# 24 of 1164 feed-forward chunks by way of ScalarE and GpSimd, and steps that run across block ends

## The chip, the core and the metric

The kernel runs on one core of a Trainium2 chip. A core has five engines with a queue each, and each works its queue in order: TensorE (PE, with its weight loads shown apart as PEld), VectorE (DVE), ScalarE (ACT), GpSimd (POOL) and SyncE (SP, which here only starts transfers). Work passes between them by semaphores. Matmul results land in PSUM, which has 8 banks of 512 float32 values per partition; GpSimd works on SBUF alone here. The metric is the time of one execution in device microseconds; "the time before" is the median of several executions.

## What is computed

`x` has 4 batches of 12416 rows of 128 values. The first half is attention by way of 32 inducing rows, the second a gated feed-forward layer with 1536 hidden units on all 49664 rows:

```
h   = softmax(scale * I @ x^T) @ x          # per batch: 32 rows, from all rows of x
y   = softmax(scale * x @ h^T) @ h          # per row of x: 32 weights
out = (sigmoid(y @ w_gate) * (y @ w_val)) @ w_out
```

The sigmoid is taken as `0.5 * (tanh(z / 2) + 1)`; the 0.5 is multiplied in at the output.

## The kernel before

**Stages.** A batch has 97 chunks of 128 rows, in 6 groups of 16 and one chunk left over. Stage 1 (`plan_stage1`) makes `h` of a batch: scores on PE, maximum on VectorE, exp on ScalarE, a transpose by DMA, a sum on PE; `plan_combine` joins the groups on GpSimd. Since `y` is only 32 weights per row times `h`, the kernel multiplies `h` into the two feed-forward weights once per batch (`hw`, 32 rows instead of 128, four copies on the four groups of 32 rows of the array). Stage 2 (`plan_stage2`) makes the 32 weights of each row of a group: scores on PE into the side bank, a copy out by ScalarE (`s2_take`, L455), the row maximum and the subtraction on GpSimd (`s2_lower_pool`, L457 to L475), exp on ScalarE (L479), and on GpSimd the sum (`s2_sum_pool`), the reciprocal (`s2_inverse_pool`) and the product `a2n` (`s2_spread`, L533); a DMA turns it (`a2r`).

**Feed-forward.** Four chunks of rows (512 columns) are a *block*: 96 blocks and one of the four left-over chunks. For each block the 1536 hidden units are taken in 12 chunks of 128 (97 x 12 = 1164 feed-forward chunks, numbered `j` in a block). A *step* has 2 or 1 of them, in turn, so a block is 8 steps; two steps, three chunks, are a *slot* here. For step `t`: `gate_fill` multiplies on PE into the gate banks, `gate` is the tanh on ScalarE from PSUM to SBUF (L809), `hidden_mm(st, "v")` fills the value banks, and the *product* on VectorE (L818) makes `u = (tanh + 1) * value` from SBUF and PSUM. `product(t)` emits the value fill of `t`, then the gate fill of `t + 2`, then the product; the product of a 2-chunk step is made to wait for the gate fill of `t + 2` (L829). A fill of a chunk has K = 32, and lies on one of four row groups by `j % 2` and by gate or value.

**Banks.** The 2-chunk step has two banks for its gate and two for its value, the 1-chunk step one and one, the output accumulator `acc` one, and all the rest (stage 1, stage 2, combining) shares the eighth, tag `m`: the side bank.

**Order.** It is written out by hand. `at(slot, make, late)` puts the work of the stages into slots: early work goes behind the first step of the slot, late work behind the second, ahead of `project`. `project` (L837) emits the output matmuls of finished products, four of 128 columns per chunk, 3 chunks in a slot, or 4 where more than 3 wait; it stops at the end of a block, where ScalarE copies the accumulator out (L865) and SP writes it (L867). Slots are counted from `base[b]`, the first of batch `b`. Buffers come from rotating pools: a tile's first writer waits for the last reader of the tile that had its buffer.

Of the kernel before, what the change touches and what calls it, by code (L numbers as in the profile page):

```python
# [9 lines left out]
F32 = mybir.dt.float32  # L10
F16 = mybir.dt.float16
BF16 = mybir.dt.bfloat16
AF = mybir.ActivationFunctionType
ALU = mybir.AluOpType
# [3 lines left out]
P = 128  # L18
# [7 lines left out]
def kernel(  # L26
# [29 lines left out]
    s1p = ctx.enter_context(tc.tile_pool(name="s1p", bufs=4))  # L56
    s2p = ctx.enter_context(tc.tile_pool(name="s2p", bufs=2))
    up = ctx.enter_context(tc.tile_pool(name="up", bufs=6))
    tp = ctx.enter_context(tc.tile_pool(name="tp", bufs=4))
    op = ctx.enter_context(tc.tile_pool(name="op", bufs=4))  # L60

# [106 lines left out]
    def at(slot, make, late=False):  # L170
        plan.setdefault((slot, late), []).append(make)
# [39 lines left out]
    def s1_exp(b, s, s1):  # L211
        ng, w, R = s1_dims(s)
        nm, l1, col = s1_col(b, s)
        a1T = s1p.tile([P, 512], F16, tag="a1T")
        nc.scalar.activation(  # L215
            out=a1T[0:R, 0 : w * P],
            in_=s1[0:R, 0 : w * P],
            func=AF.Exp,
            bias=nm[0:R, col],
            **({} if b else dict(accum_out=l1[0:R, col])),  # L220
        )
        return a1T
# [329 lines left out]
    def plan_stage2(b, c, score, take, weigh, far=None, soon=False):  # L552
        st = {}
        n = GC + (NLO if far is not None else 0)

        def bank():
            st["s2"] = ps.tile([P, GC, m], F32, tag="m", name="s2_ps")

        def room():
            st["sc"] = s2p.tile([P, GC + NLO, m], F32, tag="sc", name="sc", bufs=1)  # L560

        def one():
            room()
            bank()
            s2_score(b, 0, 0, NLO, st["s2"], True)

        def half(j0, whole):
            if j0 == 0:
                bank()
            s2_score(b, c, j0, j0 + GC // 2, st["s2"], whole)  # L570
            if soon and j0:
                st["hl"] = s2_max(GC, st["s2"])

        def lower():
            if far is None:
                room()
            s2_take(st["sc"], 0, GC, st["s2"])
            s2_lower_pool(n, st["sc"])

        def exp():  # L580
            st["e"] = s2_exp(GC, st["s2"], *st["hl"]) if soon else s2_exp_low(n, st["sc"])

        def total():
            st["sme"] = s2_sum_pool(n, st["e"])

        def spread():
            rs = (s2_inverse if soon else s2_inverse_pool)(n, st["sme"])
            st["a2n"] = s2_spread(n, st["e"][:, 0:n, :], rs, nc.gpsimd)

        def turn():  # L590
            s2_turn_dma(b, c, GC, st["a2n"], "a2r")
            if far is not None:
                s2_turn_dma(b, 0, NLO, st["a2n"], "a2l", GC)

        if far is not None:
            at(far, one)
            at(far + 1, lambda: s2_take(st["sc"], GC, NLO, st["s2"]))
        at(score, lambda: half(0, False))
        at(score + 1, lambda: half(GC // 2, not soon))
        if not soon:  # L600
            at(take, lower, late=True)
        at(weigh, exp, late=True)
        at(weigh + 1, total)
        at(weigh + 3, spread)
        at(weigh + (5 if soon else 8 if far is None else 7), turn)
# [160 lines left out]
    s2_turn_dma(0, NLO + 2 * BC, GC - 2 * BC, a2n_c, "a2r")  # L766


    steps = []
    blocks = []  # L770
    first_step = {}
    for b in range(B):
        for s in range(NG):
            first_step[(b, s)] = len(blocks) * 2 * NJ // 3
            blocks += [[(b, groups[s][0] + k, BC)] for k in range(0, GC, BC)]
    blocks.append([(b, 0, NLO) for b in range(B)])
    for i in range(len(blocks)):
        for j in range(0, NJ, 3):
            steps.append(dict(block=i, j0=j, cnt=2))
            steps.append(dict(block=i, j0=j + 2, cnt=1))  # L780
    NST = len(steps)

    def hidden_mm(st, what):
        pt = ps.tile([P, st["cnt"], 512], F32, tag=f"{what}{st['cnt']}", name=f"{what}_ps")
        for k in range(st["cnt"]):
            j = st["j0"] + k
            r = 32 * (j % 2 + (2 if what == "v" else 0))
            col = 0
            for b, c, nb in blocks[st["block"]]:
                a2r, o = a2[(b, c)]  # L790
                st[what + "end"] = nc.tensor.matmul(  # L791
                    pt[:, k, col : col + nb * P],
                    hw[b][r : r + 32, j // 2, :],
                    a2r[r : r + 32, o : o + nb, :].rearrange("p j t -> p (j t)"),
                    start=True,
                    stop=True,
                )
                col += nb * P
        st[what] = pt

    def gate_fill(t):
# [9 lines left out]
    def product(t):  # L811
# [14 lines left out]
        if st["cnt"] == 2 and 4 <= t < NST - 2:  # L826
# [3 lines left out]
                u.ins, steps[t + 2]["gend"].ins.name, AFTER, reason="tanh, gate fill, product"  # L830
            )

    acc = [None]
    queue = [(t, k) for t in range(NST) for k in range(steps[t]["cnt"])]
    queue.reverse()

    def project(upto, now, room):  # L837
        while queue and queue[-1][0] < upto and room > 0:
            t, k = queue.pop()
            st = steps[t]  # L840
            j = st["j0"] + k
            if j == 0:
                acc[0] = [ps.tile([P, BC, C], F32, tag="acc", name="acc_ps")]
                if st["block"] == len(blocks) - 1:
                    acc[0].append(ps.tile([P, BC, C], F32, tag="m", name="acc_ps"))
            for i in range(BC):
                nc.tensor.matmul(  # L847
                    acc[0][(i // 2) % len(acc[0])][:, i, :],
                    st["u"][:, k, ts(i, P)],
                    wo16[:, j, :],  # L850
                    start=(j == 0 and i in ((0, 2) if len(acc[0]) > 1 else (0,))),
                    stop=(j == NJ - 1),
                    skip_group_check=True,
                )
            room -= 1
            if t == NST - 1:
                o32 = op.tile([P, BC, C], F32, tag="o32")
                nc.scalar.mul(out=o32[:, 0:2], in_=acc[0][0][:, 0:2], mul=0.5)
                nc.sync.dma_start(ov0[:, 0, 0:2, :], o32[:, 0:2])
                nc.vector.tensor_scalar_mul(out=o32[:, 2:4], in0=acc[0][1][:, 2:4], scalar1=0.5)  # L860
                nc.scalar.dma_start(ov0[:, 0, 2:4, :], o32[:, 2:4])
            elif j == NJ - 1:
                block = blocks[st["block"]]
                o32 = op.tile([P, BC, C], F32, tag="o32")
                nc.scalar.mul(out=o32[:], in_=acc[0][0][:], mul=0.5)  # L865
                b, c, nb = block[0]
                nc.sync.dma_start(ov[b, :, c : c + nb, :], o32[:])  # L867
                if now < NST:
                    return


    base = [first_step[(b, 0)] // 2 for b in range(B)]
    for b in range(B):
        o = base[b]
        more = b + 1 < B

        if b == 0:
            plan_stage2(0, groups[1][0], o, None, o + 3, soon=True)
            plan_stage2(0, groups[2][0], o + 5, o + 7, o + 18)
        for s in range(3 if b == 0 else 2, NG - 1):  # L880
            k = o + 16 * s - 28
            plan_stage2(b, groups[s][0], k, k + 2, k + (14 if more else 10))
        plan_stage2(b, groups[NG - 1][0], o + 56, o + 58, o + 66, far=o + 52)
        if not more:
            continue
        early = (
            [(9, (16, 17, 17)), (13, (18, 19, 19))]
            if b == 0
            else [(8, (15, 16, 17)), (12, (18, 19, 19))]
        )  # L890
        later = [(24, (31, 31, 31)), (28, (35, 35, 35)), (40, (47, 48, 49)), (44, (50, 51, 51))]
        for s, (score, total) in enumerate(early + later + [(32, (43, 43, 43))]):
            plan_stage1(b + 1, s, o + score, [o + e for e in total])
        plan_combine(b + 1, o + 52, o + 55, [(o + 72, o + 74), (o + 80, o + 82)])
        plan_stage2(b + 1, groups[0][0], o + 67, o + 70, o + 78)
        plan_stage2(b + 1, groups[1][0], o + 84, o + 86, o + 94)
        for g in range(NS):
            when = 3 * g if b else 5 * g if g < NG else 12
            at(o + when, lambda b=b, g=g: x_transpose_dma(b + 1, g))
            if b == 0 and 3 <= g < NG:  # L900
                at(o + (3, 14, 17)[g - 3], lambda g=g: x_load(1, g))
        if b + 2 < B:
            for g in range(NG):
                at(o + (24, 33, 42, 60, 60, 82)[g], lambda b=b, g=g: x_load(b + 2, g))
# [56 lines left out]
```

## Time and profile before

| | |
|---|---|
| median of 3 runs | 729.52 us (729.26 to 730.78) |
| profiled execution, span from first to last instruction | 728.4 us |
| product, 1024 columns | 388 instructions, 1208 ns mean |
| product, 512 columns | 387, 673 ns |
| tanh, 1024 and 512 columns | 388 of 1032 ns, 388 of 606 ns |
| output copy, 128x512 | 96, 607 ns |
| GpSimd a2n, 128x2048 | 19, 3610 ns |
| GpSimd reciprocal (pow), 128x16 | 18, 2935 ns |
| VectorE's idle time in front of its products | 5.1 us |
| ScalarE's idle time in front of its tanh | 33.3 us |

A row of the page's groups reads: line, engine, operation, output<-inputs, shapes, count, then busy time and mean of one, then the idle time of the engine just before them with what ended it. A row of the timeline reads: start, length, engine, line, operation, count, and in brackets the idle time before it with its releaser. A row of the stretches has the stretch, its length, the busy time (and count) of PE, PEld, DVE, ACT and POOL, then the granted clock of TensorE, the DMA share and the GB/s. Records of one engine overlap by some 0.1 us, since a record begins before the one ahead of it has drained: the distance between starts tells what an instruction costs, not the record's length.

### The profile page before, as it was taken

To read this page: it belongs to the slowest core of one execution; us is meant where nothing else is said; L and a number is where in the kernel's file an instruction comes from. 1 tells how busy PE (TensorE), PEld (TensorE's weight loads), DVE (VectorE), ACT (ScalarE), POOL (GpSimd) and SP (SyncE) were. 2 spreads that over 40 slices of the span, in tenths; PEclk is the share of its full clock that TensorE was granted. 3 is DMA by queue.
4 is the path that set the end of the run, shared out by engine and by line. 5 is a ranking of instruction groups with operands and counts; after the bars stand their busy time and mean duration, and the time that the engine had idled before them with its cause. 6 is when DMAs were issued, how large, how long until landed. Compare 5 with 4: busy or idle time off the path is not lost.

```text
span 728.4 us, 21430 instructions
## 1 busy us (share of the span) xinstructions
PE 645.6 (89%) x8406; PEld 392.7 (54%) x8406; DVE 706.0 (97%) x873; ACT 675.1 (93%) x1011; POOL 419.0 (58%) x702
## 2 busy tenths in 40 slices
PE   6798888999998989999988989999999899898887
PEld 4354555555555555555555555555555555555555
DVE  3898999999999999999999999999999999999998
ACT  4688999999999999999999999999999999999996
POOL 3553836688764548488757275387865665636200
PEclk9799999999999999999999999999999999999999
DMA  9899565143547372326169530320222122121211
GB/s 172 145 161 201 98 118 103 45 103 90 91 100 168 68 147 67 81 60 133 48 114 162 103 90 31 87 69 36 75 60 74 45 60 68 43 67 45 60 45 45
DMA packets 117749, 65.19 MB, mean 89 GB/s; under 512 B 101360, under 2 KB 102032, under 8 KB 117648
## 3 DMA queue, kind: packets, MB, share of 16 engines
q1 hardware_dynamic: 111936, 49.81, 30.4%
q0 software_dynamic: 5440, 13.90, 11.2%
q8 instruction: 65, 1.06, 0.6%
q14 instruction: 36, 0.29, 0.2%
q10 hardware_dynamic: 272, 0.13, 0.1%
HBM read 27.80 MB, written 25.43 MB: 73 GB/s over the span
## 4 chain that ended last, share of the span: by engine, by line
DVE 55%; issue 24%; PE 11%; ACT 5%; DMA 3%; DVEq 1%; POOL 0%; ACTq 0%; POOLq 0%
DVE u L818 53%; ACT t L809 5%; PE acc_ps L847 4%; PE v_ps L791 3%; DMA a<-a1T 2%; DVE nm L202 2%; PE xt_ps L612 1%; DVEq L818 1%; DMA xn<-in_x_dram 1%; PE hp_ps L250 1%; PE s_ps L190 0%; PE g_ps L791 0%; ACT a1T L215 0%; PE s_ps L418 0%; PE aT_ps L228 0%
## 5 line engine op out<-in xcount | busy, mean ns | idle before, releaser
L818 DVE SCALAR_TENSOR_TENSOR u<-t,v_ps 128x1024 f16<-128x1024 f16 (+1 forms) x777 | 675.5, 939 | 5.1 <-PE g_ps L791 4.7
L809 ACT ACTIVATE t<-g_ps 128x1024 f16<-128x1024 f32 (+1 forms) x776 | 593.7, 819 | 33.3 <-ACT t L809 17.5
L791 PE MATMUL v_ps<-a2r,hwt 32*128 32x512 f16 (+1 forms) x1188 | 294.4, 372 | 65.6 <-DVE u L818 64.6
L847 PE MATMUL acc_ps<-wo,u 128*128 128x128 f16 x4656 | 329.6, 221 | 0.0
L847 PEld LDWEIGHTS <-u 128*128 128x128 f16 x4656 | 262.8, 98 | 88.8 <-issue 87.8
L791 PE MATMUL g_ps<-a2r,hwt 32*128 32x512 f16 (+1 forms) x1188 | 297.5, 378 | 0.0
L791 PEld LDWEIGHTS <-hwt 32*128 32x128 f16 x2400 | 91.1, 91 | 197.7 <-issue 153.4
L487 POOL TENSOR_TENSOR sum<-e 128x256 f32<-128x256 f16 (+1 forms) x23 | 15.4, 671 | 148.2 <-ACT e L479 144.2
L533 POOL TENSOR_TENSOR a2n<-e,rs 128x2048 f16<-128x2048 f16 (+2 forms) x24 | 86.2, 3593 | 6.7 <-PE g_ps L791 2.8
L511 POOL TENSOR_TENSOR near<-sme,minus 128x16 f32<-128x16 f32 (+1 forms) x22 | 65.2, 2963 | 1.8
L865 ACT ACTIVATE o<-acc_ps 128x512 f32<-128x512 f32 x96 | 58.3, 607 | 0.0
L466 POOL TENSOR_SCALAR rise<-rise 128x256 f32<-128x256 f32 (+6 forms) x110 | 51.1, 464 | 9.7
L465 POOL TENSOR_TENSOR rise<-sc 128x256 f32<-128x256 f32 (+1 forms) x22 | 16.2, 738 | 38.9 <-ACT sc L455 38.7
L467 POOL TENSOR_TENSOR top<-top,rise 128x128 f32<-128x128 f32 (+3 forms) x88 | 28.3, 321 | 7.3
L487 POOL TENSOR_TENSOR sum<-sum 128x128 f32<-128x128 f32 (+3 forms) x92 | 28.3, 307 | 7.2
L465 POOL TENSOR_TENSOR rise<-top 128x128 f32<-128x128 f32 (+3 forms) x88 | 27.1, 308 | 6.9
L470 POOL TENSOR_TENSOR sc<-sc,top 128x512 f32<-128x512 f32 (+1 forms) x22 | 23.9, 1084 | 1.7
L418 PEld LDWEIGHTS <-xT 128*128 128x128 f16 x388 | 13.4, 97 | 12.2 <-issue 12.2
L418 PE MATMUL s_ps<-hT,xT 128*128 128x32 f16 x388 | 18.2, 179 | 0.3 <-DVE hT L315 0.3
L467 POOL TENSOR_TENSOR top<-sc,rise 128x256 f32<-128x256 f32 (+1 forms) x22 | 16.3, 740 | 1.8
L250 PE MATMUL hp_ps<-xn,a 128*32 128x128 f16 x388 | 14.2, 225 | 2.9 <-DMA a<-a1T 2.6
L215 ACT ACTIVATE a1T<-s_ps,nm 128x512 f16<-128x512 f32 (+1 forms) x24 | 15.1, 628 | 1.7 <-DVE nm L202 1.7
(118 smaller groups left out, 235.9 us busy)
## 6 DMA issues: line engine op xcount, KB each, us to landing
out_dram<-o SPq DMA_DIRECT2D x96, 256.0 KB, 2.3
xn<-in_x_dram POOLq DMA_DIRECT2D x19, 512.0 KB, 8.1
xn<-in_x_dram POOLq DMA_DIRECT2D x4, 544.0 KB, 6.3
a2r<-a2n SPq DMA_TRANSPOSE x29, 4.4
xn<-in_x_dram POOLq DMA_DIRECT2D x1, 384.0 KB, 14.6
wg<-in_moe_w_gate_dram POOLq DMA_DIRECT2D x1, 384.0 KB, 4.4
wv<-in_moe_w_val_dram POOLq DMA_DIRECT2D x1, 384.0 KB, 5.4
wo<-in_moe_w_out_dram POOLq DMA_DIRECT2D x1, 384.0 KB, 5.5
```

The costliest lines, as they stand in the source:

```text
L418: nc.tensor.matmul(s2[:, j, :], xT[b][:, c + j, :], hT16[b][:], start=(j == 0), stop=whole and j == j1 - 1, skip_group_check=True,)
L465: nc.gpsimd.tensor_tensor(out=r, in0=far, in1=near, op=ALU.subtract)
L466: nc.gpsimd.tensor_scalar_max(out=r, in0=r, scalar1=0.0)
L467: nc.gpsimd.tensor_tensor(out=top[:, 0:n, 0:w], in0=near, in1=r, op=ALU.add)
L487: nc.gpsimd.tensor_tensor(out=d[:, 0:n, :], in0=src[:, :, 0:w], in1=src[:, :, w : 2 * w], op=ALU.add)
L511: nc.gpsimd.tensor_tensor(out=near[:, 0:n], in0=sme[:, 0:n], in1=minus1[:, 0:n], op=ALU.pow)
L533: eng.tensor_tensor(out=a2n[:, 0:n, :, :], in0=e.unsqueeze(2).to_broadcast((P, n, 4, m)), in1=rs.unsqueeze(2).unsqueeze(3).to_broadcast((P ...
L791: st[what + "end"] = nc.tensor.matmul(pt[:, k, col : col + nb * P], hw[b][r : r + 32, j // 2, :], a2r[r : r + 32, o : o + nb, :].rearrange ...
L809: st["tanh"] = nc.scalar.activation(out=st["t"][:], in_=st["g"][:], func=AF.Tanh, scale=0.5)
L818: u = nc.vector.scalar_tensor_tensor(out=st["u"][:, :, c:e], in0=st["t"][:, :, c:e], scalar=1.0, in1=st["v"][:, :, c:e], op0=ALU.add, op1= ...
L847: nc.tensor.matmul(acc[0][(i // 2) % len(acc[0])][:, i, :], st["u"][:, k, ts(i, P)], wo16[:, j, :], start=(j == 0 and i in ((0, 2) if len( ...
L865: nc.scalar.mul(out=o32[:], in_=acc[0][0][:], mul=0.5)
```

## The change

24 chunks leave the steps. For each, `plan_aside` puts a gate fill into the side bank at one slot, a tanh to a float32 tile `tx` on ScalarE and an addition of 1 on GpSimd (late in that slot); at a second slot a value fill into the side bank, a copy to a float32 tile `vx` on ScalarE and a product on GpSimd to a tile `ux`. `tx` and `vx` have one buffer each, `ux` two. The projection of such a chunk comes at the end of its block. Of the 24, 3, 4, 4 and 13 are in the four batches; `aside` lists (gate slot, value slot, block from the batch's first). The steps then take the remaining 1140 chunks in order, three to a slot, whatever block they are in, and the slots of the stages are counted from the shifted starts of the batches (0, 95, 190, 284 in place of 0, 96, 192, 288). The pools of tanh tiles, output tiles and `a1T` go from 4 buffers to 3.

```diff
-    tp = ctx.enter_context(tc.tile_pool(name="tp", bufs=4))
-    op = ctx.enter_context(tc.tile_pool(name="op", bufs=4))
+    tp = ctx.enter_context(tc.tile_pool(name="tp", bufs=3))
+    op = ctx.enter_context(tc.tile_pool(name="op", bufs=3))
+    xp = ctx.enter_context(tc.tile_pool(name="xp", bufs=2))
...
-        a1T = s1p.tile([P, 512], F16, tag="a1T")
+        a1T = s1p.tile([P, 512], F16, tag="a1T", bufs=3)
...
+    usual = [(60, 65, 17), (76, 88, 23), (90, 92, 24)]
+    aside = [
+        list(usual),
+        [(0, 2, 2)] + usual,
+        [(0, 2, 2)] + usual,
+        [(0, 2, 2), (8, 10, 3), (16, 18, 6), (24, 26, 7), (32, 34, 10), (40, 42, 11)]
+        + [(48, 50, 14), (60, 62, 17), (68, 70, 19), (72, 74, 19), (77, 79, 21), (81, 83, 22)]
+        + [(85, 87, 23)],
+    ]
+    kept = [NJ] * len(blocks)
+    for b in range(B):
+        for k, (g, v, i) in enumerate(aside[b]):
+            kept[first_block[(b, 0)] + i] -= 1
...
-    for i in range(len(blocks)):
-        for j in range(0, NJ, 3):
-            steps.append(dict(block=i, j0=j, cnt=2))
-            steps.append(dict(block=i, j0=j + 2, cnt=1))
+    chunks = [(i, j) for i in range(len(blocks)) for j in range(kept[i])]
+    steps = []
+    for k in range(0, len(chunks), 3):
+        steps.append(dict(chunks=chunks[k : k + 2], cnt=2))
+        steps.append(dict(chunks=chunks[k + 2 : k + 3], cnt=1))
...
+    def plan_aside(gate_slot, value_slot, i, j):
+        st = {}
+
+        def fill(what):
+            st[what] = ps.tile([P, 512], F32, tag="m", name=f"side_{what}")
+            hidden_chunk(st[what][:], i, j, what)
+
+        def gate_take():
+            st["t"] = xp.tile([P, 512], F32, tag="tx", name="tx", bufs=1)
+            nc.scalar.activation(out=st["t"][:], in_=st["g"][:], func=AF.Tanh, scale=0.5)
+            nc.gpsimd.tensor_scalar_add(out=st["t"][:], in0=st["t"][:], scalar1=1.0)
+
+        def value_take():
+            v = xp.tile([P, 512], F32, tag="vx", name="vx", bufs=1)
+            nc.scalar.copy(out=v[:], in_=st["v"][:])
+            uside[(i, j)] = xp.tile([P, 512], F16, tag="ux", name="ux16")
+            nc.gpsimd.tensor_tensor(
+                out=uside[(i, j)][:], in0=st["t"][:], in1=v[:], op=ALU.mult
+            )
+
+        at(gate_slot, lambda: fill("g"))
+        at(gate_slot, gate_take, late=True)
+        at(value_slot, lambda: fill("v"))
+        at(value_slot, value_take, late=True)
...
-    queue = [(t, k) for t in range(NST) for k in range(steps[t]["cnt"])]
+    queue = []
+    for t in range(NST):
+        for k, (i, j) in enumerate(steps[t]["chunks"]):
+            queue.append((t, k, i, j))
+            if j == kept[i] - 1:
+                queue += [(t, None, i, e) for e in range(kept[i], NJ)]
...
+        for g, v, i, j in aside[b]:
+            plan_aside(o + g, o + v, i, j)
```

`hidden_chunk` is the inner loop of `hidden_mm`, taken out: one matmul for each part of the block, of one chunk `j`.

## The prediction

> **What bounds the kernel now.** I read the engine shares and the chain of waits of the page, then the groups by shape, then the timeline of single instructions around 409 us. A *slot* is two steps, three chunks: one product of 1024 columns and one of 512.
>
> ```profile
> PE 645.6 (89%) x8406; PEld 392.7 (54%) x8406; DVE 706.0 (97%) x873; ACT 675.1 (93%) x1011; POOL 419.0 (58%) x702
> ...
> DVE 55%; issue 24%; PE 11%; ACT 5%; DMA 3%; DVEq 1%; POOL 0%; ACTq 0%; POOLq 0%
> ...
> L818 DVE SCALAR_TENSOR_TENSOR u<-t,v_ps 128x1024 f16<-128x1024 f16 x388 | 468.5, 1208 | 3.4 <-PE g_ps L791 3.0
> L818 DVE SCALAR_TENSOR_TENSOR u<-t,v_ps 128x512 f16<-128x512 f16 x387 | 260.4, 673 | 1.7 <-PE g_ps L791 1.7
> ...
> 407.49 1.20 DVE L818 SCALAR_TENSOR_TENSOR u<-t,v_ps 128x1024 f16<-128x1024 f16 x1
> ...
> 409.22 1.20 DVE L818 SCALAR_TENSOR_TENSOR u<-t,v_ps 128x1024 f16<-128x1024 f16 x1
> ...
> 408.75 0.39 PE L791 MATMUL v_ps<-a2r,hwt 32*128 32x512 f16 x2
> 409.35 0.37 PE L791 MATMUL v_ps<-a2r,hwt 32*128 32x512 f16 x1
> 409.67 0.84 PE L847 MATMUL acc_ps<-wo,u 128*128 128x128 f16 x12
> 410.48 0.39 PE L791 MATMUL v_ps<-a2r,hwt 32*128 32x512 f16 x2
> ...
> 409.66 0.67 PEld L847 LDWEIGHTS <-u 128*128 128x128 f16 x12 [0.23 <-issue]
> 410.44 0.14 PEld L791 LDWEIGHTS <-hwt 32*128 32x128 f16 x5
> ...
> 409.24 1.51 ACT L809 ACTIVATE t<-g_ps 128x1024 f16<-128x1024 f32 x2 [0.21 <-ACT t L809]
> 410.64 0.60 ACT L865 ACTIVATE o<-acc_ps 128x512 f32<-128x512 f32 x1
> 411.12 1.04 ACT L809 ACTIVATE t<-g_ps 128x1024 f16<-128x1024 f32 x1
> ```
>
> VectorE looks like the bound at 97%. The single rows show that it is one member of a ring. The 1024-column product starts at 407.49 and ends at 408.69; only then can PE refill its bank pair (408.75, 0.39 us, with the gate fill of the next step beside it), and the next such product starts at 409.22. One turn is 409.22 - 407.49 = 1.73 us, and 388 turns are 671 us of the 728.4. Nothing in this ring runs ahead: a delay of PE or of ScalarE at the fill is added to the end and is not won back. How near the two are to delaying it: PE's last projection weights are in at 409.66 + 0.67 = 410.33 and the fill's weights load at 410.44, so PE has 0.11 us to spare in a slot. ScalarE ends its tanh at about 409.24 + 1.03 = 410.27 and the fill that waits for it starts at 410.48: 0.21 us. One output copy (410.64) pushes the next tanh from 409.24 + 1.73 = 410.97 to 411.12, which these 0.21 us still hide.
>
> **What is gained.** 24 chunks are 8 slots (the changed program has 380 of the 1024-column products, not 388): 8 x 1.73 = 13.8 us. No other term shortens the ring, so this is all there is to win.
>
> **GpSimd's queue, and one buffer.** The side chunk's tanh goes into tx, of which there is one; it is free when GpSimd has multiplied the chunk before. Counted in slots from a batch's base, every batch but the last has a side chunk with gate 76 and value 88, and the next gate at 90. In GpSimd's order that multiply stands behind the row maximum of the group whose scores ScalarE copies out in slot 86. In the second batch that stretch is:
>
> ```profile
> 365.17 0.72 POOL L465 TENSOR_TENSOR rise<-sc 128x256 f32<-128x256 f32 x1 [3.05 <-ACT sc L455]
> ...
> 372.68 1.07 POOL L470 TENSOR_TENSOR sc<-sc,top 128x512 f32<-128x512 f32 x1
> ...
> 371.73 1.51 ACT L809 ACTIVATE t<-g_ps 128x1024 f16<-128x1024 f32 x2 [0.21 <-ACT t L809]
> ```
>
> GpSimd is taken until 373.75. The multiply has no row of its own: between 1.07 (the 128x512 row above) and 2 x 0.73 = 1.46 (twice 128x256); I take 1.2, so tx is free at 375.05. ScalarE reaches the tanh of slot 90 just before the pair at 371.73, at about 371.4; a delay in slot 88 (below) makes it 371.8. It waits 3.2 us with every later tanh behind it; less the 0.2 to spare, 3.0 us, in three batches: 9.0. In the last batch the gates at 68 and 72 meet the same: add (one input, 128x512: between 0.86, the 128x256 row, and 1.72; I take 1.6), then the spread of 7.9 us that ran from 670.16 to 678.06, then the multiply. From the late place of slot 68 (670.2) this is 0.6 + 1.6 + 7.9 + 1.2, with gaps 681.6, against a tanh wanted at 677.1 plus 0.6 of delays: 3.9 us, less 0.2, 3.7. Together +12.7 (10 to 15). The last group's a2n also ends some 2.5 us later, and its transpose and the output writes behind it on SP with it; the stall gives the time back.
>
> **The clock after such a wait.** At 67.5 PE waited for a transpose:
>
> ```profile
> 69.37 0.24 PE L250 MATMUL hp_ps<-xn,a 128*32 128x128 f16 x4 [1.81 <-DMA a<-a1T]
> ...
> 71.84 1.82 DVE L818 SCALAR_TENSOR_TENSOR u<-t,v_ps 128x1024 f16<-128x1024 f16 x2 [1.03 <-PE g_ps L791]
> 74.29 6.41 DVE L818 SCALAR_TENSOR_TENSOR u<-t,v_ps 128x1024 f16<-128x1024 f16 x7 [0.63 <-PE g_ps L791]
> ...
> 70.00:72.00 2.00, 2.00 (x34) 1.36 (x32) 0.84 (x2) 1.22 (x3) 0.66 (x1) 0.55 1.15 294
> ```
>
> The granted clock (the 0.55) fell for some 3 us, and VectorE lost 1.03 + 0.63 = 1.66 us more after the wait was over. Four waits could cost 0 to 6.6; I take half, +3.3. [...]
>
> **PE's projections.** Before, every slot projects 3 chunks (12 matmuls). With blocks of 11 the block ends no longer fall on slot ends; the projection stops at a block's end and takes 4 in a later slot. In the changed program's order 100 of 380 slots hold 16 matmuls. Four more at 0.67/12 = 0.057 are 0.23 us, against 0.11 to spare: 0.12 to 0.23, and 0.15 taken, since the fill can follow somewhat closer. A slot right after one that paid is nearly free, because its 512-column fill then comes earlier against the late product: 70 of the 100 pay. 13 of them follow on a slot with doubled ScalarE work, where the larger delay counts. 57 x 0.15 = +8.6 (0 to 13).
>
> **ScalarE, twice in a slot.** 48 more instructions of about 0.48 (410.64 to 411.12). One in a slot is hidden like the output copy. But in 20 slots two such stand together (a side tanh or copy with an output copy in most, an exp or a score copy in three); before, none did. The tanh is then 0.15 + 0.48 = 0.63 late, 0.21 is hidden: 20 x 0.42 = +8.4 (0 to 11, with side copies in neighbouring slots).
>
> **Smaller.** Seven 2-chunk steps pair chunks with the same row group, so that their two fills may queue: 512 columns at 0.057 per 128 are 0.23, once for the gate and once for the value, 0 to 3.2; I take 1.5. Side fills stand between the two fills of a slot, where PE idles from 409.14 to 409.35; the sixteen matmuls that stood there at 409.08 moved no product, so 0 (up to 48 x 0.1). A side product is projected at its block's end, at the nearest some two slots after its multiply: 0. The pools cut to 3 buffers: one output tile in 6.9 us, landing in 2.3, and tanh tiles that are read within two slots; 0.
>
> **Sum.** -13.8 + 12.7 + 3.3 + 8.6 + 8.4 + 1.5 = +20.7. The profiled span is 728.4, 1.1 under the median of 729.52, so I add to the median: 750.
>
> **Rivals.** *PE and ScalarE absorb the crowding* (the records have 53 us of ScalarE idle, and the spare of a slot may be larger than these rows tell): then only GpSimd's queue and part of the clock are left, -13.8 + 12.7 + 0 to 6.6: 728 to 735. Against it: of the slots without other VectorE work nearly all take 1.73 and none less, and lateness past 0.2 shows up. 18%. *The buffer is free in time* (faster): tx is the point; if the multiply is done within 0.5 us of slot 90, ScalarE has no wait, VectorE's 13.8 stay and half of the crowding is paid: -13.8 + 0 to 10, 716 to 726. For it: GpSimd is only 58% busy. Against it: its place behind an 8.6 us run. 10%. *The clock falls at every wait and slows the crowded slots after it*: all upper ends, 763 to 775. 7%. That the chunks aren't moved is excluded by the program's order.
>
> **Numbers.** The forecast has 65% and 736 to 762. Under 732 I leave the faster case and half of the first rival, over 762 the third and little else: range 732 to 762. Within 0.2% (1.5 us, about what the spread of the three runs allows) only the first rival's lower end: 5%. Faster 10%, slower 85%.
>
> **What would show it.** In the changed profile: ScalarE's side tanh with idle time of about 3 us put down to GpSimd, four times; clock dips right behind; slots of 1.73 us where 12 matmuls stand and about 1.88 where 16 do; 2.15 after a doubled slot; VectorE's idle before its product up from 5 us to over 25. It is wrong if the 16-matmul slots stay at 1.73, or the multiply runs ahead of the row maximum.

## The result, and the profile after

The changed kernel takes 776.15 us (median of four runs, 775.04 to 778.98) where the kernel before took 730.15 beside it (729.26 to 738.89): 1.0604 times as long, 95% interval 1.0522 to 1.0686. The forecast was 750, the range 732 to 762. The direction held; the size did not: 46 us were lost where 20.5 had been forecast.

The kernel before itself takes 728 to 730 us in some executions and 734 to 739 in others, so kernels are set against 729 below, while the ratios in brackets are against those executions, of either kind, that were taken beside each kernel.

First the engine shares, the granted clock in 40 slices and the costliest groups of the page after.

```profile
span 773.2 us, 21511 instructions
PE 669.9 (87%) x8406; PEld 409.0 (53%) x8406; DVE 702.9 (91%) x857; ACT 686.1 (89%) x1043; POOL 484.1 (63%) x750
PEclk9699999899989999979989999999999999999899
...
L873 ACT ACTIVATE tx<-side_g 128x512 f32<-128x512 f32 x24 | 14.7, 613 | 12.7 <-POOL ux L880 12.7
L874 POOL TENSOR_SCALAR tx<-tx 128x512 f32<-128x512 f32 x24 | 35.9, 1495 | 21.1 <-ACT tx L873 20.9
L880 POOL TENSOR_TENSOR ux<-tx,vx 128x512 f16<-128x512 f32 x24 | 30.4, 1268 | 23.7 <-issue 21.4
```

The same two product groups by shape as before, now at line 846:

```profile
L846 DVE SCALAR_TENSOR_TENSOR u<-t,v_ps 128x1024 f16<-128x1024 f16 x380 | 462.1, 1216 | 47.1 <-PE g_ps L813 26.4 <-PE v_ps L813 7.2 <-PE side_v L813 6.3
L846 DVE SCALAR_TENSOR_TENSOR u<-t,v_ps 128x512 f16<-128x512 f16 x379 | 257.2, 679 | 5.6 <-PE g_ps L813 3.1 <-PE v_ps L813 2.5
```

The eight products are gone (380, not 388) and one takes nearly as long as before (1216 ns against 1208). But VectorE now stands idle 47.1 us before the 1024-column products, against 3.4, so its share falls from 97% to 91% while the span grows. Of the clock slices five are below 9 behind the second one, spread over the whole kernel; before there was none behind the second. GpSimd's two new rows are 1495 and 1268 ns; the prediction had taken 1.6 and 1.2.

The table of all waits after (engine, line, what ended the wait: total us, times, longest) tells what VectorE waits behind:

```profile
DVE u L846 <- PE g_ps L813: 29.5, 48, 1.6
...
ACT tx L873 <- POOL ux L880: 12.7, 4, 3.7
PE g_ps L813 <- ACT t L837: 12.3, 5, 3.4
...
PE side_g L813 <- DMA a2r<-a2n: 5.8, 3, 2.1
```

The second row is the wait that was forecast: four times, 12.7 us. The last row was in no term of the sum. The first adds up what follows from a late or slow PE.

To book the time I took, in the profile, the distance between the starts of successive 1024-column products, less the 1.73 us of an undisturbed turn, less the other VectorE work between them. From slot 20 on this excess is 2.2 us before and 60.3 after. With the 13.8 that the eight slots gain: -13.8 + 60.3 - 2.2 = +44.3; the two spans differ by 773.2 - 728.4 = 44.8. So the excess is nearly all of it. It parts as follows; each entry is the whole excess of the slots named, which is a little more than the waits alone (12.7 and 5.8 in the table of waits):

| what stands at the slot | forecast | measured, us |
|---|---|---|
| ScalarE waits for `tx` (slots 91, 186, 281, 357) | 12.7 | 3.24 + 2.99 + 3.24 + 4.02 = 13.5 |
| PE waits for `a2r` at a side gate (slots 60, 155, 250) | 0 | 3.31 + 1.59 + 1.59 = 6.5 |
| half clock in the slots behind (15 windows of 3.41 us) | 3.3 | about 16 |
| slots with 16 projection matmuls, and their neighbours | 8.6 | about 17 |
| slots with ScalarE's work doubled | 8.4 | about 7.5 |
| same row group | 1.5 | not seen apart |

**The wait for `tx`**, second batch, in the timeline (start us, us, engine, what, in brackets the wait before it):

```profile
207.84 1.07 POOL L471 TENSOR_TENSOR sc<-sc,top 128x512 f32<-128x512 f32 x1
208.88 1.26 POOL L880 TENSOR_TENSOR ux<-tx,vx 128x512 f16<-128x512 f32 x1
210.17 0.60 ACT L873 ACTIVATE tx<-side_g 128x512 f32<-128x512 f32 x1 [2.93 <-POOL ux L880]
211.73 0.61 PE L813 MATMUL g_ps<-a2r,hwt 32*128 32x512 f16 x2 [2.66 <-ACT t L837]
```

The multiply stands behind the row maximum's last row, as the prediction read from the order of GpSimd's queue; the tanh starts 0.03 us after it ends, and PE's next gate fill waits 2.66 us for the ring's tanh behind it. That fill takes 0.61 us, not 0.39: the granted clock is one half in the two stretches from 210.7 on.

**The wait for `a2r`**, at slot 60:

```profile
141.24 3.61 POOL L534 TENSOR_TENSOR a2n<-e,rs 128x2048 f16<-128x2048 f16 x1
...
144.87 1.78 SPq L545 DMA_TRANSPOSE a2r<-a2n  x1
...
149.24 0.58 PE L813 MATMUL side_g<-a2r,hwt 32*128 32x512 f16 x1 [2.11 <-DMA a2r<-a2n]
149.97 0.69 DVE L846 SCALAR_TENSOR_TENSOR u<-t,v_ps 128x512 f16<-128x512 f16 x1 [1.55 <-PE v_ps L813]
```

The side gate of slot 60 is of block 17, whose own steps begin at slot 17 x 12 / 3 = 68. The rows read from top to bottom: GpSimd's spread ends at 144.85, the transpose is issued 0.02 us later and takes 4.3 us to land, and the fill starts at 149.24. It had stood at the head of PE's queue for 2.11 us with the ring's value fill behind it, and VectorE waited for that one.

The profile before had this transpose at the same place:

```profile
144.96 1.78 SPq L544 DMA_TRANSPOSE a2r<-a2n  x1
```

There it lands at 149.29, and those of the same group of the second and third batch at 319.74 and 490.19. The first product of the batch's slot 60 starts at 147.29, 317.74 and 488.32: the transposes land 2.0, 2.0 and 1.9 us behind it, 5.9 in all, and the changed kernel waited 2.1, 2.0 and 1.7. Before, nothing read these tiles until the blocks' own steps, slots later. So the wait could have been read ahead of the run.

**What a wait leaves behind.** The same place in stretches of 3.41 us (columns: busy us and instructions of PE, PEld, VectorE, ScalarE, GpSimd; then the granted clock, DMA share, GB/s):

```profile
142.38:145.79 3.41, 3.01 (x38) 1.78 (x36) 3.41 (x5) 3.36 (x6) 3.41 (x2) 1.00 0.23 82
145.79:149.20 3.41, 1.34 (x18) 0.83 (x17) 2.62 (x3) 2.41 (x3) 3.05 (x5) 1.00 0.80 154
149.20:152.61 3.41, 3.37 (x22) 1.50 (x22) 1.06 (x2) 2.00 (x4) 3.01 (x5) 0.51 0.01 2
152.61:156.03 3.42, 3.42 (x30) 2.48 (x30) 2.88 (x4) 2.57 (x4) 2.76 (x9) 0.50 0.20 77
156.03:159.44 3.41, 3.25 (x39) 2.02 (x37) 3.16 (x5) 2.38 (x4) 3.14 (x7) 0.99 0.00 0
```

In the second stretch PE is busy for 1.34 of 3.41 us. The clock then is one half for two stretches, in which PE is busy all the time and gets through 22 and 30 instructions. VectorE is busy for 1.06 of the first of them: the wait is over and the ring still loses time, since the two slots with 12 matmuls that lie wholly at half clock take 2.36 and 2.39 us (slots 61 and 157), and those with 16 take 3.1 to 3.2. After slot 50 there are 15 such stretches, at slots 60, 91, 155, 172, 187, 231, 250, 282 and 357; about 16 us of excess lie in them outside the waits, 1.1 each. That is booked by place; no run takes the clock away by itself.

**ScalarE twice in a slot** (ring tanh last in the row):

```profile
181.39 0.61 ACT L873 ACTIVATE tx<-side_g 128x512 f32<-128x512 f32 x1
181.87 0.62 ACT L926 ACTIVATE o<-acc_ps 128x512 f32<-128x512 f32 x1
182.34 3.19 ACT L837 ACTIVATE t<-g_ps 128x1024 f16<-128x1024 f32 x4
...
183.97 2.97 DVE L846 SCALAR_TENSOR_TENSOR u<-t,v_ps 128x1024 f16<-128x1024 f16 x3 [0.47 <-PE g_ps L813]
```

The tanh starts 0.95 us after the side tanh (182.34 - 181.39), and VectorE waits 0.47.

### The profile page after: what moved, and what is told of

The parts are those of the page before. It is cut to its first block, busy times and chain, and to the rows that moved or that the text cites. A ratio compares the mean times of both kernels' runs of the same rounds, so it can differ in the third digit from the quotient of the medians.

```text
span 773.2 us, 21511 instructions
## 1 busy us (share of the span) xinstructions
PE 669.9 (87%) x8406; PEld 409.0 (53%) x8406; DVE 702.9 (91%) x857; ACT 686.1 (89%) x1043; POOL 484.1 (63%) x750
## 3 DMA queue, kind: packets, MB, share of 16 engines
q8 instruction: 65, 1.06, 0.6%
## 5 line engine op out<-in xcount | busy, mean ns | idle before, releaser
L846 DVE SCALAR_TENSOR_TENSOR u<-t,v_ps 128x1024 f16<-128x1024 f16 x761 | 672.4, 946 | 52.7 <-PE g_ps L813 29.5
L837 ACT ACTIVATE t<-g_ps 128x1024 f16<-128x1024 f32 x760 | 584.8, 824 | 53.8 <-ACT t L837 26.9
L908 PE MATMUL acc_ps<-wo,u 128*128 128x128 f16 x4560 | 334.9, 226 | 5.5 <-ACT o L926 4.6
L908 PEld LDWEIGHTS <-u 128*128 128x128 f16 x4560 | 271.0, 101 | 107.1 <-issue 105.3
L813 PEld LDWEIGHTS <-hwt 32*128 32x128 f16 x2400 | 94.2, 91 | 206.6 <-issue 155.7
L874 POOL TENSOR_SCALAR tx<-tx 128x512 f32<-128x512 f32 x24 | 35.9, 1495 | 21.1 <-ACT tx L873 20.9
L880 POOL TENSOR_TENSOR ux<-tx,vx 128x512 f16<-128x512 f32 x24 | 30.4, 1268 | 23.7 <-issue 21.4
L873 ACT ACTIVATE tx<-side_g 128x512 f32<-128x512 f32 x24 | 14.7, 613 | 12.7 <-POOL ux L880 12.7
```

The lines of the kernel that those rows point to most:

```text
L813: end = nc.tensor.matmul(dst[:, col : col + nb * P], hw[b][r : r + 32, j // 2, :], a2r[r : r + 32, o : o + nb, :].rearrange("p j t -> p (j ...
L837: st["tanh"] = nc.scalar.activation(out=st["t"][:], in_=st["g"][:], func=AF.Tanh, scale=0.5)
L846: u = nc.vector.scalar_tensor_tensor(out=st["u"][:, :, c:e], in0=st["t"][:, :, c:e], scalar=1.0, in1=st["v"][:, :, c:e], op0=ALU.add, op1= ...
L874: nc.gpsimd.tensor_scalar_add(out=st["t"][:], in0=st["t"][:], scalar1=1.0)
L908: nc.tensor.matmul(acc[0][(q // 2) % len(acc[0])][:, q, :], u[:, ts(q, P)], wo16[:, j, :], start=(j == 0 and q in ((0, 2) if len(acc[0]) > ...
```

## The experiments

The theory after the result: five separate delays as in the table, each of the size given there. The rival: the distances between products are long for one common reason (ScalarE and GpSimd too full), and taking a single wait away only shows the next one.

**One wait at a time.** The first kernel gives `tx` two buffers (in float16, so that they fit), the second moves the side gate of slot 60 in the first three batches one slot later, the third has both edits.

```diff
-            st["t"] = xp.tile([P, 512], F32, tag="tx", name="tx", bufs=1)
+            st["t"] = xp.tile([P, 512], F16, tag="tx", name="tx", bufs=2)
```

> The changed kernel with two buffers for the side tanh (float16 instead of float32, so that they fit). Theory (a ledger of the changed kernel's slots: four waits of ScalarE for GpSimd's multiply cost 13.5 us and the half-clock stretches behind them 7.2): both go, 776 to 755 (752 to 760), with the copy of slot 74 perhaps still 1 us late for its own single buffer. Rival (the waits only hide another lateness, which comes out next): above 768.

```diff
-    usual = [(60, 65, 17), (76, 88, 23), (90, 92, 24)]
+    usual = [(61, 65, 17), (76, 88, 23), (90, 92, 24)]
```

> The changed kernel with the gate slot 60 of the first three batches moved to 61, since in slot 60 PE waited for the transposed weights of block 17's group. Theory: the three waits (6.5 us) and the half clock behind them (6.1) go, 776 to 764 (761 to 767). Rival (the transpose is needed then anyway, or the wait moves to the next fill): above 772.

> The changed kernel with both mends at once: two buffers for the side tanh and gate slot 61. Theory (the two kinds of wait are apart in time and add): 776 less 15.5 less 6 to 12, so 748 to 754; what is left over the 734 without side work is doubled ScalarE slots (8 us) and half-clock windows. Rival (each mend only lets the other's lateness show): above 757.

Measured: 760.67 us (759.4 and 761.9; 1.031 times the kernel before, 1.027 to 1.035), 770.67 (767.8 and 773.5; 1.044, 1.035 to 1.054) and 750.19 (746.7 and 753.6; 1.023, 1.004 to 1.042). In the tables of waits the first has no wait of ScalarE for `tx` left, and the wait for `a2r` as large as ever:

```profile
PE side_g L813 <- DMA a2r<-a2n: 6.4, 3, 2.6
```

and the second the reverse, with the wait for `a2r` down to 2.6 us in all and this one unchanged to the tenth:

```profile
ACT tx L873 <- POOL ux L880: 12.7, 4, 3.7
```

So these are two waits and not one. The first is worth 776.15 - 760.67 = 15.5 us, the second 5.5, both 26.0: more than their sum of 21.0, by less than the two times of the third kernel differ. New waits show in that kernel, at slot 76 (1.6 us of excess) and at 359 (1.9), so the rival has a point: the next ones are smaller, but they do come. The first kernel came just outside its 752 to 760: the wait at slot 359 stands in its profile too, and a stretch at half clock at slot 219 (1.5 us of excess), neither of them in the changed kernel's. Its edit also changes the type of `tx`; no run has the second buffer without that, so the 15.5 us are of both together. The second gave less than expected (770.67 against 761 to 767): of its 2.6 us, 0.8 stand at slot 156, where one slot was not enough for a fill that had waited 2.0, and 1.3 at slot 76, where the next side gate now waits for its own transpose, with a stretch at half clock behind it.

**No side work.** The 24 chunks are still projected, but from a constant tile: their fills, tanhs, copies and GpSimd work are left out.

```diff
+    still = xp.tile([P, 512], F16, tag="ux", name="ux16")
+    nc.gpsimd.memset(still[:], 0.0)
...
-        at(gate_slot, lambda: fill("g"))
-        at(gate_slot, gate_take, late=True)
-        at(value_slot, lambda: fill("v"))
-        at(value_slot, value_take, late=True)
+        uside[(i, j)] = still
```

> The changed kernel without the side work: the fills, tanh, copies and GpSimd operations of the 24 chunks are left out, and a constant stands for their products; steps, blocks and projections stay. Theory: what is left is the gain of 8 slots (-13.8) and the uneven projections (49 first slots of 16 matmuls at 0.17 to 0.23 and 35 following ones, about 14.6, and a few us of half clock): 730 to 737. Rival (the side work is the whole loss, PE has room): 716 to 719.

Measured: 734.03 us (732.9 to 734.4; 0.999, 0.987 to 1.010). The clock stays whole from slot 3 to the last (0.988 in the mean of the profile, as in the kernel before), and the excess is 19.0 us. 729 - 13.8 + 19.0 - 2.2 = 732.0, against 732.92 in the profiled execution. Everything that VectorE was to be spared is spared here, at no cost to another engine but PE, and nothing is won: PE's uneven slots take the 13.8 back: in this profile 71 of the 100 slots with 16 matmuls pay, 14.7 us in all, and of the other 4 us some stands in the slots right behind them. The side work itself costs 776.15 - 734.03 = 42 us.

**The price of a slot with 16 matmuls**, in the kernel before with nothing else changed: its projections, 3 chunks in every slot, are dealt as 1, 4, 4, 3 and as 2, 4, 3, 3.

```diff
-            project(t - 1, t, 3 if waiting(t - 1) <= 3 else 4)
+            project(t - 1, t, (3, 1, 4, 4)[(t // 2) % 4])
```

The second kernel has `(3, 2, 4, 3)` there.

> The kernel before, with its projections dealt unevenly, 1, 4, 4 and 3 chunks in the four slots of a block in place of 3 each. Theory: the first slot of 16 matmuls costs 0.17, the second is free, 96 x 0.17 = 16: 746; if slots of one chunk also let the clock fall, each fall adds some 1.5 us: 750 to 790. Rival (PE absorbs it): 729 to 732.

> The kernel before with its projections dealt 2, 4, 3 and 3 in the four slots of a block. Theory: 96 slots of 16 matmuls at 0.17 each and no slot so empty that the clock falls: 745 to 748, with as few half-clock windows as before. Rival (the 36 us that the 1, 4, 4, 3 deal cost were the matmuls of the full slots alone, and the clock has no part): about half of 36, or all of it, with windows of half clock here too.

Measured: 765.54 us (761.9 and 769.2; 1.037, 1.026 to 1.049) and 754.04 (748.9 and 759.2; 1.029, 1.006 to 1.051). The second's timeline of PE around one slot of 16:

```profile
602.05 0.39 PE L791 MATMUL v_ps<-a2r,hwt 32*128 32x512 f16 x2
603.78 0.39 PE L791 MATMUL v_ps<-a2r,hwt 32*128 32x512 f16 x2 [0.16 <-DVE u L818]
...
604.70 1.07 PE L847 MATMUL acc_ps<-wo,u 128*128 128x128 f16 x16
605.70 0.39 PE L791 MATMUL v_ps<-a2r,hwt 32*128 32x512 f16 x2
...
607.42 0.39 PE L791 MATMUL v_ps<-a2r,hwt 32*128 32x512 f16 x2
```

From value fill to value fill it takes 1.73, 1.92 and 1.72 us. The slot with 16 costs 0.19 here, 0.18 in the median of both kernels; the next one gives nothing back, and the lighter slot before it nothing either. In the first kernel the second 16 of a pair costs nearly nothing (1.736 us in the median). A quarter of the slots paying 0.18 would be 97 x 0.18 = 17.5 us, so 746; the second kernel comes near that (748.9 in the profiled execution, with two stretches at half clock after slot 50, where the kernel before has none), though its median lies above the 745 to 748 that had been expected; the first took 765. What it has besides is time at half clock: five stretches of 3.41 us at one half about slots 18 and 30, and six from slot 54 on. Those six come without any engine of the ring having waited long (PE at most 0.77 us at once, VectorE and ScalarE 0.02 at most). One of them:

```profile
244.68:248.09 3.41, 3.40 (x47) 1.99 (x44) 3.31 (x4) 2.79 (x5) 1.55 (x3) 1.00 0.88 170
248.09:251.50 3.41, 2.03 (x22) 0.84 (x19) 3.41 (x6) 3.39 (x7) 0.00 (x0) 1.00 0.63 156
251.50:254.92 3.42, 3.42 (x42) 2.21 (x41) 2.29 (x3) 1.97 (x3) 0.00 (x0) 0.50 0.93 81
```

In the middle stretch VectorE is busy throughout. PE, which got one chunk in one of its slots in place of three, is busy for 2.03 of 3.41 us, and the clock falls at its end.

**The price of ScalarE's second piece**, in the kernel before: the output copy of every second block is made twice (a spare tile, and three output buffers to make room for it).

```diff
+                if st["block"] % 2:
+                    nc.scalar.mul(out=spare[:], in_=acc[0][0][:], mul=0.5)
```

> The kernel before with the output copy of every second block made a second time into a spare tile, so that 48 slots hold two ScalarE instructions of 0.48 us. Theory: the next tanh is 0.63 us late, about 0.2 of it is hidden: 48 x 0.42 to 0.55, 750 to 756. Rival (ScalarE's idle time of 33 us in front of its tanh takes them up): 729 to 732.

Measured: 746.50 us (746.35 and 746.65; 1.018, 1.003 to 1.034), and from slot 50 on 31 slots with 0.44 to 0.47 of excess:

```profile
373.58 0.60 ACT L866 ACTIVATE o<-acc_ps 128x512 f32<-128x512 f32 x1
374.06 0.62 ACT L868 ACTIVATE spare<-acc_ps 128x512 f32<-128x512 f32 x1
374.53 3.09 ACT L809 ACTIVATE t<-g_ps 128x1024 f16<-128x1024 f32 x4
...
376.07 2.95 DVE L818 SCALAR_TENSOR_TENSOR u<-t,v_ps 128x1024 f16<-128x1024 f16 x3 [0.38 <-PE g_ps L791]
```

The first piece is hidden, the second is not: 0.42 in the prediction, 0.46 here. Expected were 750 to 756 and 746.5 came: 33 of the 48 slots paid from slot 20 on.

**Fewer of the uneven slots.** If PE's unevenness eats the gain, taking the chunks in threes from one block should keep the block ends on slot ends and bring the gain out. Eight blocks lose three chunks each; no side work is done, as above. The second kernel takes the last batch's threes from other blocks, and the third also leaves the projections of the 24 chunks out.

```diff
-    usual = [(60, 65, 17), (76, 88, 23), (90, 92, 24)]
+    usual = [(0, 0, 17)] * 3
...
-        [(0, 2, 2), (8, 10, 3), (16, 18, 6), ...
+        [(0, 0, i) for i in (6, 10, 14, 18, 22) for _ in range(3)],
```

> As the kernel without side work, but the 24 chunks are taken three at a time from 8 blocks, so that every block still ends on a slot's end and no step runs across one. The side work is left out here as well. Theory (the loss of the kernel without side work is the uneven projections, and these come from the block ends): 729.5 less 13.8 plus 8 x 0.35 to 0.5, so 717 to 721, 13 to 17 below the 734 of the other. Rival (the 4 chunks in a slot are what costs, wherever the blocks end): 726 or more.

```diff
-        [(0, 0, i) for i in (6, 10, 14, 18, 22) for _ in range(3)],
+        [(0, 0, i) for i in (2, 20, 21, 22, 23) for _ in range(3)],
```

> As the kernel with 24 chunks taken three at a time, side work left out again, but with the last batch's five blocks put where no group comes more than one slot ahead of its transpose until the end (blocks 2 and 20 to 23). Theory (each of the 27 slots with 16 matmuls that does not follow a paying one costs 0.18): 729.5 less 13.8 plus 3 to 4, 718 to 720.

> The same with the 24 chunks' projections left out too, so that PE has 12 matmuls in every slot. Theory (what the removal of product work cannot win is PE's share of these chunks, which stays and is squeezed into fewer slots): the whole 13.8, 715 to 717, and 3 to 4 below the run with them. Rival (VectorE's products were not the bound to this extent, or PE's projections are free): both runs alike, within 1 us.

Measured: 726.71 us (725.4 to 736.8; 0.993, 0.986 to 0.999), 721.72 (720.4 to 729.4; 0.986, 0.974 to 0.997) and 718.61 (717.5 to 725.0; 0.982, 0.971 to 0.992). The first missed its 717 to 721; the other two came 1.7 and 1.6 us above their 718 to 720 and 715 to 717. In the first one's profile, an execution of 736.75 us with 8 us of its excess ahead of slot 35, PE waits for the last group's transpose at slot 359; the second kernel takes that wait away. Before the last group's first block, near block 20 of its batch, the first kernel has taken out four threes, the second kernel a single one. The second therefore needs that transpose 9 chunks, 3 slots, 5.2 us later, and there is no excess at slot 359 in its profile. The third is 3.1 us below the second (excess 4.3 against 7.9): the projections of the 24 chunks, at 0.17 to 0.22 in 17 slots of 16, are what parts the two. Without them nearly the whole gain is there: its profiled span is 715.7, and 728.4 - 13.8 = 714.6. The pools cut to 3 buffers have no run of their own, but this kernel has them too, so they cost it little.

**Other slots for the side work.** Could the full work be placed so that no wait is left? Side gates were moved back, to where their transposes should have landed, and multiplies ahead of the row maximum, in all batches, then with 12 chunks of the last batch alone.

```diff
-    usual = [(60, 65, 17), (76, 88, 23), (90, 92, 24)]
+    usual = [(61, 65, 17), (77, 83, 23), (89, 91, 24)]
...
-        + [(48, 50, 14), (60, 62, 17), (68, 70, 19), (72, 74, 19), (77, 79, 21), (81, 83, 22)]
-        + [(85, 87, 23)],
+        + [(48, 50, 14), (60, 61, 17), (68, 69, 19), (76, 77, 20), (79, 80, 21), (82, 83, 22)]
+        + [(86, 87, 23)],
```

> The changed kernel with its list of slots alone rewritten, so that no side fill comes ahead of its transposed weights (gates 61 and 77), no multiply stands behind a row maximum that holds the tanh buffer (value 83 for 88, 69 for 70, the four last pairs in consecutive slots), and almost no side instruction shares a slot with an output copy. Theory (the loss is these three and the uneven projections, and nothing else): the 734 of the kernel without side work plus 1 to 5 us for side instructions in the slot after an output copy, 735 to 740, without half clock after slot 50. Rival (the side work costs ScalarE, GpSimd or the side bank something that the ledger has not found): 745 or more.

> The same list, but only 12 chunks, all of the last batch, leave the steps. Theory: 4 slots less is 6.9 us; 24 slots of 16 matmuls, some 19 of them paying 0.18, and a few tight slots give back 3.5 to 5: 727 to 729 against 729.5, so a gain at the edge of what can be told. Rival (side work costs more than the ledger says): 732 or more.

Both missed, and both times came where the rival had them (745 or more, 732 or more). Measured: 756.77 us (750.0 to 761.3; 1.031, 1.022 to 1.040) and 741.77 (734.6 to 744.8; 1.013, 1.003 to 1.023). The first waits at slot 89 (3.1 us of excess) for the transpose that block 24's side gate reads, at 184 (1.4), and at 359 for the last group, which is no side work at all:

```profile
706.44 3.64 SPq L545 DMA_TRANSPOSE a2r<-a2n  x2
...
708.90 0.39 PE L813 MATMUL g_ps<-a2r,hwt 32*128 32x512 f16 x1
710.17 0.53 SPq L928 DMA_DIRECT2D out_dram<-o  x1
710.74 0.37 PE L813 MATMUL g_ps<-a2r,hwt 32*128 32x512 f16 x1 [1.45 <-DMA a2r<-a2n]
```

The gate fill at 710.74 belongs to an ordinary step. The second kernel, with 12 chunks in the last batch alone, has the same wait at slots 363 to 365 (excess 1.98 + 1.08 + 0.56), which is half of the 6.9 us that its four slots can gain.

The rest can be read from the excess. Of the 42.1 us of the first, 8.0 stand at slots 20 to 32, ahead of its first side gate in slot 61, and about 9 at these three waits and behind them. The other 25 are some 6 more than the 19.0 of the kernel without side work. Of the 17.9 of the second, 5.0 stand at slots 31 and 32, long before its side work in the last batch, and 3.6 at slots 363 to 365; the other 9.3, where 3.5 to 5 had been expected, alone exceed the 6.9. What they consist of was not followed up. No version that does the whole work beat the kernel before.

## Why the prediction was wrong, step by step

- **What bounds the kernel, and "8 x 1.73 = 13.8 us":** right. There are 380 products at nearly the same duration, and the kernel without side work and without the extra projections comes to 718.6.
- **GpSimd's queue and `tx`, +12.7:** right in place, cause and size (13.5), and not by luck: the parts agree one by one (3.24, 2.99 and 3.24 for 3.0, 4.02 for 3.7). The run with a second buffer confirms it, -15.5 with the clock behind it.
- **"Side fills stand between the two fills of a slot ... so 0":** this step failed. It asked whether PE has room for the fill, and not whether its input is there. A side gate reads `a2r` eight slots ahead of its block's own steps, and the transpose landed 1.7 to 2.1 us after PE had come to the fill, as the profile before could tell. The table has 6.5 us of wait, and 6.1 of half clock behind it: 12.6 us where nothing had been put. The run that moves this gate by one slot wins 5.5 of them back, and 10.5 on top of the second buffer.
- **"The stall gives the time back"** (the last group's transpose): true only as long as the stall stands ahead of it. In the run with both waits mended an excess of 1.87 us appears at slot 359, and the threes show why: every chunk taken out brings the following blocks forward by 0.58 us, and the stage that feeds them does not come forward with them.
- **The clock after a wait, +3.3, half of 0 to 6.6:** this term failed by its size, which was off by a factor of five; that the clock falls behind a wait was right. About 16 us, of which 7.2 behind the `tx` waits (the upper bound, 6.6, was the better value), 6.1 behind the `a2r` waits that had been missed, and 2.7 at slots 172 and 231, where nothing waited long (PE at most 0.8 us). That the clock may also fall because of uneven slots was in no step; the dealing 1, 4, 4, 3 shows it by itself, with six stretches at one half from slot 54 on. Whether that is what happened at slots 172 and 231 stays open: the kernel without side work has the same uneven slots and no fall there.
- **Slots with 16 matmuls, 57 x 0.15 = +8.6:** the count of 100, of which 70 pay, was right (71 of 100 in the kernel without side work) and the price slightly low (0.18 in the median, 0.3 to 0.5 in eight of them). What had no term are the slots beside them, some of which pay 0.15 to 0.2 as well. Of the 17 us, the first slots of a run come to 10.4, further ones to 2.1, and their neighbours to 4.9.
- **ScalarE twice in a slot, 20 x 0.42 = +8.4:** right (about 7.5 us in all, 0.46 each in the kernel made for it).
- **Same row group, +1.5:** not seen apart from the rest; left open.
- **Rivals:** "absorb" and "the buffer is free in time" fell, the first by the 0.18 and 0.46 that the slots pay, the second by the 3.2 us waits. The third, 763 to 775, with 7%, was nearest. Its range was worked out with all upper ends of the terms that were there; the measured 776 has the missed wait in it besides.

The forecast sum was +20.7 and the profiles have +44.3. Of the 23.6 us between them 6.5 are the missed wait, 16 - 3.3 = 12.7 the clock and 17 - 8.6 = 8.4 the slots of 16; the smaller terms, with the 2.2 of excess that the kernel before has itself, take off the 4.0 that this is too much. The range missed because its upper end, 762, was made of the terms that were there: an input that arrives late, and the clock behind it and in uneven slots, had no bound in it.

## What to carry to other kernels

Work taken from the engine that looks like the bound shortens the kernel only by what the whole ring loses: here PE kept the projections and ScalarE and GpSimd got more, and with the side work left out altogether the kernel still gained nothing until PE's slots were made even. When work is moved earlier, look up when its inputs land as well as whether the engine has room, and do the same for everything that comes forward because work was removed ahead of it. And price a wait of PE, or an uneven slot, with the slots at half clock that can follow it (here 15 stretches of 3.41 us, about 1.1 us lost in each), not by its own length.

## What the runs showed of the hardware

In the profiles before and after, the granted clock falls first at 25.81 and 26.36 us from the span's start. From there to the last matmul every change of it, 4 and 22 with the first, lies a whole number of times 3.413 us from the first one (after: 149.24, 156.07, 210.68, 217.51 us and so on), and whenever it is not whole it is one half, for 1 to 4 such stretches.

Whether the clock falls went with the time that PE was busy in the stretch just ahead (by the rows' own ends). Of the 13 falls, two before and eleven after, eleven stand behind a stretch in which PE was busy for 0.28 to 1.87 us of 3.41, and two behind 2.48 and 2.27 (at 367.70 and 483.75 us, slots 172 and 231). The other 383 stretches at whole clock, from the one ahead of the first fall on, had PE busy for 2.25 us or more, and no fall behind them. In the run with 1, 4, 4, 3, the fall at 251.50 us stands behind a stretch in which PE was busy for 2.03 of 3.41 us and waited for at most 0.77 us at once. What parts the two behind 2.27 and 2.48 us from the stretches of 2.25 to 2.55 us in the same profile that no fall followed, these runs do not tell.
